# Head-row transfers of a stacked key/query tile: rows r, r+6, r+12, ... instead of sixteen neighbouring rows

## The chip, the cores and the metric

The kernel runs on one core of a Trainium2 chip. The metric is device time in microseconds (us) of one execution, as the median over several runs. Beside it there is one profiled execution, whose trace gives the start and length of every instruction and of every transfer. Engines are named as in the trace: PE (TensorE matmuls), PEld (TensorE weight loads), DVE (VectorE), ACT (ScalarE), POOL (GpSimd), SP (the queue from which most transfers are issued).

## The reference

Two parts run one after the other. The first is an attention with a complex decay: per batch (4) and head (8) a 48x48 complex state is carried over 768 steps. The second is a mixture of experts in which 3072 tokens are given to 8 experts, 384 tokens each, in the order of their gate logits.

```
mag = sqrt(a_re*a_re + a_im*a_im); scale = minimum(mag, 0.999) / (mag + 1e-06)
a_re_n, a_im_n = a_re * scale, a_im * scale
for t in range(S):                      # S = 768, per batch and head, D = 48
    new_re = ar * S_re - ai * S_im
    new_im = ar * S_im + ai * S_re
    S_re, S_im = new_re + outer(k[t], v[t]), new_im
    y[t] = q[t] @ S_re
x = y as [B*S, H*D]                     # 3072 x 384
logits = x @ w_gate; every token goes to its best expert that has room (384 each)
out[mask_e] = relu(x[mask_e] @ w1[e]) @ w2[e]
```

## The kernel before

The attention is computed in chunks of 128 steps. Three chunks are a group, two groups a batch, and there are eight groups (24 chunks). ACT and DVE first turn a group's decays into logarithms, running sums, and sines and cosines of the running angle (tile `CS`); keys and queries are scaled by the running decay (tile `kq`).

For each chunk, DVE then multiplies keys and queries by cosine and sine (`RK`, `RQ` in `turns`) and writes the result into tile `f`. In `f` a partition is one of 16 features and one of 8 heads (partition 8d+h), and along the partition lie 3 feature blocks x 2 (cosine part, sine part), each with 128 key columns, 128 query columns and one column `P0` with the decay of the whole chunk: 257 columns a chunk.

TensorE needs something else: for each head all 96 features (3 blocks x 2 parts x 16) along the partitions. This is tile `KQ`, 96 partitions x 8 heads x 257 columns per chunk. `stack` makes it with six transfers from on-chip memory to on-chip memory, issued on SP. Transfer r takes block r//2, part r%2 of all 128 partitions of `f` and puts it into 16 rows of `KQ`, each row holding its 8 heads one behind the other; this document calls it a head-row transfer. A group's three chunks are stacked in two packs: one chunk alone (six transfers of 16x8x257 elements) and the other two together (six of 16x8x514); in the last group the pack of two comes first. So there are 16 packs and 96 head-row transfers. `f` for a pack of two has one buffer, `KQ` has two.

Every reader of `KQ` either sums over its 96 rows or carries them along: `sc` (scores, key columns times query columns), `kp` (the key columns turned by TensorE, copied by ACT to `kt`, which makes the state update `U`), `W` (the state, `U` times the gate column, 96 rows), and the second half of `y` (state times query columns). DVE masks `sc` into `am`, and `am` times `V` is the first half of `y`. `xT`, `xp` and `x` bring `y` into token rows, which ACT's queue stores in DRAM (`xd`).

The order of the instructions on each engine is fixed ahead: `in_order` plays the list of operations through with estimated durations and emits them in that order; `hot` matmuls fill gaps in PE's estimated time. Each engine, and SP's queue, works in that order and waits where an operand is not there. A transfer on SP also waits for the transfer that used the same one of eight completion counters before it. The second part, the experts, begins after the last chunk and contains no head-row transfer.

Of the kernel before, what the change touches and what calls it, by code (L numbers as in the profile page):

```python
# [236 lines left out]
def attention(nc, real, tc, z, q, k, a_re, a_im, v_tok, xd, later):  # L237
# [29 lines left out]
    def op(key, eng, cost, prio, fn, deps=()):  # L267
        kind = key[0][0] if type(key[0]) is tuple else key[0]
        o = Op(eng, cost, fn, [made.get(d) for d in deps], prio)
        o.kind = kind + ("<" if prio < EARLY else ">" if prio >= LATE else "")  # L270
        if kind in LAGS:
            o.wait, o.lag = LAGS[kind]
        ops.append(o)
        made[key] = o
        return o

    def dve(n):
        return n / 960 + 0.1
# [19 lines left out]
    tiles = {}  # L298

    def get(name, gi, shape=None, p=ew, **kw):  # L300
        if (name, gi) not in tiles:
            tiles[name, gi] = p.tile(shape or [128, 3, T], F32, name=name, **kw)
        return tiles[name, gi]
# [128 lines left out]
    def pack(i):  # L432
        k = next(k for k, m in packs.items() if i in m)
        return k, i - packs[k][0], len(packs[k]), packs[k]

    def before(k, n):
        same = [x for x in packs if len(packs[x]) == len(packs[k])]
        at = same.index(k) - n
        return same[at] if at >= 0 else None

    def turns(i):

        gi, c = i // GC, i % GC
        piece = next(j for j, (lo, hi) in enumerate(cuts[gi]) if lo <= c < hi)
        t = slice(c * 128, c * 128 + 128)

        def X(*stages):
            return [(s_, gi, piece) for s_ in stages]

        pk, at, n, mates = pack(i)  # L450

        def ftile():
            return get(f"f{n}", pk, [128, 3, 2, n * 257], bufs=F_BUFS[n])[..., 257 * at:257 * at + 257]

        f_free = [("K", before(pk, F_BUFS[n]))]
        op(("P0", i), "dve", 0.1, i, lambda: v.tensor_copy(
            ftile()[..., 256], tiles["gc", gi][:, :, c, None].to_broadcast([128, 3, 2])), X("G4") + f_free)
        for m, name in enumerate(("RK", "RQ")):
            def rot(m=m):
                v.tensor_tensor(ftile()[..., 128 * m:128 * m + 128],  # L460
                                get("kq", gi)[:, m, :, t][:, :, None].to_broadcast([128, 3, 2, 128]),
                                tiles["CS", gi][..., t], op=OP.mult)
            op((name, i), "dve", dve(768), i, rot, X("T1", "T3", "G3" if m else "G5") + f_free)

        if at < n - 1:
            return

        def stack():
            KQ = get(f"KQ{n}", pk, [96, 8, n * 257], p=st, bufs=KC_BUFS[n])
            for r in range(6):  # L470
                nc.sync.dma_start(KQ[16 * r:16 * r + 16], tiles[f"f{n}", pk][:, r // 2, r % 2])
        deps = [(x, m) for m in mates for x in ("RK", "RQ", "P0")]
        for m in packs.get(before(pk, KC_BUFS[n]), ()):
            deps += [("MX", m), ("FL", m, 0), ("FL", m, 1), ("WM", m)]
        op(("K", pk), "dma", K_COST[n], i, stack, deps)

    nu = G * GC
# [970 lines left out]
```

## Time and profile before

| | |
|---|---|
| median of 3 runs | 640.8 us (640.6 to 641.47) |
| profiled execution, its own time | 643.34 us |
| its span, first to last instruction | 641.6 us |
| attention stage, from the first head-row transfer to the last state update | 38.7 to 347 us |
| experts | from about 347 us to the end |
| busy over the span | PE 81%, DVE 66%, ACT 43%, POOL 13% |
| mean granted TensorE clock | 0.846 of full speed |

The span is the profiled execution's; around it lie 1.7 us of the profiled execution's time. Shares of busy time over the whole span mix the two stages; the stage with the head-row transfers is the first.

### The profile page before, as it was taken

Reading aid. Unit: us, or ns where it says so; the run is one execution under the profiler, and the core shown is the slowest. Engines: PE = TensorE matmul, PEld = TensorE weight load, DVE = VectorE, ACT = ScalarE, POOL = GpSimd, SP = SyncE. Lnnn points to the kernel's source line nnn. Section 1 sums busy time; section 2 is a strip of 40 time slices with the busy share of each in tenths; the row PEclk is TensorE's granted clock in tenths of the full one; section 3 lists DMA queues with packets and bytes.
Section 4 is the critical chain, followed back from the end, with each engine's and each line's share of the span. In section 5 each row is a group of like instructions: output and inputs, shape, how many; then the busy total and the mean of one; then the engine's idle time right before and its main releaser. Section 6 shows DMA issues by size and latency. Waiting matters only on the chain.

```text
span 641.6 us, 9748 instructions
## 1 busy us (share of the span) xinstructions
PE 518.9 (81%) x3706; PEld 455.1 (71%) x3713; DVE 425.2 (66%) x1250; ACT 278.1 (43%) x426; POOL 84.3 (13%) x96
## 2 busy tenths in 40 slices
PE   0047988959689593987897599898999999999994
PEld 0017867757677573976786398477988898899994
DVE  8874766836658274574524757678899999895140
ACT  6882645746447372642421013323243434364140
POOL 2000000000000000000000021313323241451101
PEclk9995695956959587785859579799999999999998
DMA  8779496976969769295941154106342434391000
GB/s 260 219 104 175 111 158 194 143 192 132 153 195 135 200 139 148 95 117 93 119 68 38 35 201 186 61 25 229 111 166 104 167 120 152 134 363 46 26 13 37
DMA packets 41230, 86.04 MB, mean 134 GB/s; under 512 B 3809, under 2 KB 29921, under 8 KB 39137
## 3 DMA queue, kind: packets, MB, share of 16 engines
q1 hardware_dynamic: 31424, 42.55, 35.6%
q0 software_dynamic: 6304, 38.16, 17.9%
q10 hardware_dynamic: 3456, 4.72, 2.5%
q8 instruction: 29, 0.48, 0.3%
q14 instruction: 17, 0.13, 0.1%
HBM read 53.49 MB, written 9.44 MB: 98 GB/s over the span
## 4 chain that ended last, share of the span: by engine, by line
PE 43%; DMA 27%; DVE 12%; issue 8%; SPq 4%; ACT 3%; POOL 2%; POOLq 0%; DVEq 0%; ACTq 0%
PE acc L131 25%; DMA KQ<-f 19%; PE sc L131 5%; SPq L131 4%; PE y L131 3%; PE U L131 3%; DVE f L131 2%; PE kp L131 2%; DMA V<-in_v 2%; PE cnt L131 2%; ACT s L131 2%; PE xp L131 2%; DMA xd<-x 2%; DMA w1t<-in_w,eidx 1%; DMA s<-s 1%
## 5 line engine op out<-in xcount | busy, mean ns | idle before, releaser
L131 DVE TENSOR_TENSOR am<-sc,mask 128x512 f32<-128x512 f32 x48 | 32.7, 689 | 80.3 <-PE sc L131 80.3
L131 PE MATMUL sc<-KQ 96*128 96x128 f32 x384 | 67.6, 348 | 4.1 <-DMA KQ<-f 4.1
L131 PEld LDWEIGHTS sc<-KQ 96*128 96x128 f32 x384 | 64.4, 259 | 6.1 <-issue 5.8
L131 PE MATMUL kp<-ident,KQ 96*128 96x96 f32 x160 | 25.6, 322 | 53.0 <-DMA KQ<-f 39.1
L131 PEld LDWEIGHTS kp<-ident,KQ 96*128 96x128 f32 x160 | 22.1, 193 | 60.1 <-issue 57.4
L131 PE MATMUL hot<-cold 128*128 128x512 bf16 x113 | 28.6, 408 | 36.9 <-DVE cold L131 36.4
L131 ACT ACTIVATE hh<-acc 128x384 fp32r<-128x384 f32 x56 | 27.4, 491 | 63.2 <-PE acc L131 63.0
L131 PE MATMUL acc<-w2l,hh 128*128 128x384 f32 x168 | 54.1, 346 | 0.0
L131 PE MATMUL acc<-w2h,hh 128*128 128x384 f32 x168 | 53.7, 345 | 0.0
L131 PE MATMUL acc<-w2h,hl 128*128 128x384 f32 x168 | 53.5, 343 | 0.0
L131 PE MATMUL acc<-xl,w1h 128*128 128x384 f32 x168 | 51.4, 344 | 0.0
L131 PE MATMUL acc<-xh,w1h 128*128 128x384 f32 x168 | 51.3, 345 | 0.0
L131 PE MATMUL acc<-xh,w1l 128*128 128x384 f32 x168 | 51.2, 344 | 0.0
L131 PEld LDWEIGHTS <-cold 128*128 128x128 bf16 x120 | 12.6, 105 | 51.0 <-issue 35.7
L131 PE MATMUL y<-am,V 128*64 128x128 f32 x384 | 45.9, 337 | 0.0
L131 POOL DMA_INDIRECT out<-ot,idx x24 | 30.6, 1273 | 116.2 <-ACT ot L131 106.0
L131 PEld LDWEIGHTS U<-V,kt 128*96 128x96 f32 x320 | 41.9, 223 | 2.4 <-issue 1.9
L131 DVE TENSOR_TENSOR f<-kq,CS 128x768 f32<-128x768 f32 x48 | 42.6, 951 | 0.5 <-ACT CS L131 0.5
L131 PE MATMUL U<-V,kt 128*96 128x48 f32 x320 | 41.9, 301 | 1.0 <-DVE W L131 1.0
L131 ACT ACTIVATE kt<-kp 128x384 f32<-128x384 f32 x40 | 18.9, 489 | 54.7 <-PE kp L131 53.5
L131 DVE SCALAR_TENSOR_TENSOR hl<-acc,hh 128x384 fp32r<-128x384 f32 x56 | 30.4, 551 | 17.8 <-ACT hh L131 17.1
L131 DVE TENSOR_TENSOR ind<-m,thr 128x768 bf16<-128x768 f32 (+1 forms) x40 | 33.7, 848 | 8.5 <-PE thr L131 8.1
(198 smaller groups left out, 1179.7 us busy)
## 6 DMA issues: line engine op xcount, KB each, us to landing
KQ<-f SPq DMA_DIRECT2D x48, 257.0 KB, 10.6
KQ<-f SPq DMA_DIRECT2D x48, 128.5 KB, 4.6
V<-in_v SPq DMA_DIRECT2D x8, 576.0 KB, 13.8
kq<-in_k SPq DMA_DIRECT2D x8, 576.0 KB, 8.2
kq<-in_q SPq DMA_DIRECT2D x8, 576.0 KB, 8.4
xd<-x ACTq DMA_DIRECT2D x24, 192.0 KB, 3.5
ai<-in_a_im SPq DMA_DIRECT2D x6, 576.0 KB, 4.5
ar<-in_a_re SPq DMA_DIRECT2D x6, 576.0 KB, 3.9
```

The lines of the kernel that those rows point to most:

```text
L131: r = f(*a, **k)
```

## The change

The row order of `KQ` within a head changes. Transfer r wrote the 16 neighbouring rows 16r to 16r+15; now it writes the rows r, r+6, r+12, ..., r+90. Its source, its size, its place in the order and the queue it is issued on stay as they are, and so does every instruction on every engine, with its waits. The readers of `KQ` use all 96 rows, so the sums run over the same terms in another order of rows, and the state's rows are in the new order too.

```
--- before
+++ after
@@ -468,7 +468,7 @@
         def stack():
             KQ = get(f"KQ{n}", pk, [96, 8, n * 257], p=st, bufs=KC_BUFS[n])
             for r in range(6):
-                nc.sync.dma_start(KQ[16 * r:16 * r + 16], tiles[f"f{n}", pk][:, r // 2, r % 2])
+                nc.sync.dma_start(KQ[r::6], tiles[f"f{n}", pk][:, r // 2, r % 2])
```

## Rows read from the trace of the kernel before

**Rows 1.** The page: the span, and the chain of work that ended last by engine and line, with shares of the span.
```profile
span 641.6 us, 9748 instructions
...
PE acc L131 25%; DMA KQ<-f 19%; PE sc L131 5%; SPq L131 4%; PE y L131 3%; PE U L131 3%; DVE f L131 2%; PE kp L131 2%; DMA V<-in_v 2%; PE cnt L131 2%; ACT s L131 2%; PE xp L131 2%; DMA xd<-x 2%; DMA w1t<-in_w,eidx 1%; DMA s<-s 1%
```

**Rows 2.** The attention stage as one stretch: its length, busy time and number of instructions of PE, PEld, DVE, ACT and POOL, the granted clock, the busy share of the DMA engines (over 1 where packets overlap), GB/s.
```profile
38.70:347.00 308.30, 248.84 (x1892) 217.07 (x1897) 178.94 (x321) 149.99 (x191) 3.37 (x4) 0.73 0.77 138
```

**Rows 3.** The chain of waits between 225 and 300 us, in order of time, from the first issue of a cycle to the landing of its pair and on to the next `f`: start, us, what.
```profile
233.28 0.55 SPq L131
...
235.82 5.15 DMA KQ<-f
...
240.99 14.85 DMA KQ<-f
...
270.59 1.90 DVE f L131 x3
```

**Rows 4.** SP's queue, one row from 192 us and then between 228 and 282 us: start, us over which the x transfers were issued, what.
```profile
191.95 9.47 SPq L131 DMA_DIRECT2D KQ<-f  x12
...
233.28 8.26 SPq L131 DMA_DIRECT2D KQ<-f  x12
...
272.50 8.34 SPq L131 DMA_DIRECT2D KQ<-f  x12
```

**Rows 5.** Everything that writes or reads tile `KQ`: the 96 issues (shortest, median, longest in ns), the time from issue to landing, and from the page the median landing of the pair's transfers (257 KB) and of the single chunk's (128.5 KB).
```profile
L131 SPq DMA_DIRECT2D KQ<-f x96: 547/597/1265, 38.7 to 330.4; - x96
...
DMA to landing us min/median/max: 3.1/5.8/16.4
...
KQ<-f SPq DMA_DIRECT2D x48, 257.0 KB, 10.6
KQ<-f SPq DMA_DIRECT2D x48, 128.5 KB, 4.6
```

**Rows 6.** Three stretches (columns as in rows 2): one in which only head-row transfers of a pack of two move beside a store, one in which only loads of `kq` and `V` move, one with those of a pack of one.
```profile
242.00:254.00 12.00, 3.78 (x33) 3.40 (x32) 5.05 (x12) 3.23 (x6) 0.00 (x0) 0.80 1.08 116
257.00:260.00 3.00, 3.00 (x18) 3.00 (x17) 0.61 (x1) 2.82 (x4) 0.00 (x0) 0.50 1.05 370
235.00:240.00 5.00, 3.96 (x36) 2.63 (x35) 5.00 (x8) 4.64 (x7) 0.00 (x0) 1.00 1.09 131
```

**Rows 7.** The packets of the first and of the last of these stretches.
```profile
DMA packets 766, 1.39 MB, mean 116 GB/s; under 512 B 89, under 2 KB 114, under 8 KB 765
DMA packets 718, 0.66 MB, mean 131 GB/s; under 512 B 79, under 2 KB 718, under 8 KB 718
```

**Rows 8.** TensorE's groups of the attention stage that waited for head-row transfers: number, busy us, mean ns, idle us of the engine before them and who ended it.
```profile
L131 PE MATMUL sc<-KQ 96*128 96x128 f32 x384 | 67.6, 348 | 4.1 <-DMA KQ<-f 4.1
L131 PE MATMUL kp<-ident,KQ 96*128 96x96 f32 x160 | 25.6, 322 | 53.0 <-DMA KQ<-f 39.1 <-DMA V<-in_v 7.9 <-issue 6.0
```

**Rows 9.** The cycle from 233 to 273 us, and one row of the next, in order of time: start, us, engine, what, and in brackets the engine's idle time before it.
```profile
244.74 1.04 PE L131 MATMUL xp<-pick,xT 112*128 112x104 f32 x8
256.08 1.51 PE L131 MATMUL kp<-ident,KQ 96*128 96x96 f32 x8 [10.30 <-DMA KQ<-f]
257.39 1.97 PE L131 MATMUL sc<-KQ 96*128 96x128 f32 x8
259.15 2.69 PE L131 MATMUL U<-V,kt 128*96 128x48 f32 x16
259.39 0.69 DVE L131 TENSOR_TENSOR am<-sc,mask 128x512 f32<-128x512 f32 x1 [11.87 <-PE sc L131]
262.60 1.35 DVE L131 TENSOR_TENSOR kq<-kq,zi 128x1152 f32<-128x1152 f32 x1
263.10 0.64 PE L131 MATMUL y<-KQ,W 96*64 96x128 f32 x4
265.38 1.28 PE L131 MATMUL U<-W,ident 96*96 96x384 f32 x2
267.58 0.69 DVE L131 TENSOR_TENSOR am<-sc,mask 128x512 f32<-128x512 f32 x1 [3.63 <-PE sc L131]
269.15 1.08 PE L131 MATMUL sc<-KQ 96*128 96x128 f32 x8
270.06 1.48 PE L131 MATMUL U<-V,kt 128*96 128x48 f32 x16
270.59 1.82 DVE L131 TENSOR_TENSOR f<-kq,CS 128x768 f32<-128x768 f32 x2
272.19 0.39 PE L131 MATMUL y<-KQ,W 96*64 96x128 f32 x4
273.39 0.89 PE L131 MATMUL U<-W,ident 96*96 96x384 f32 x2
...
281.45 0.88 PE L131 MATMUL kp<-ident,KQ 96*128 96x96 f32 x8 [2.37 <-DMA KQ<-f]
```

**Rows 10.** Stretches of 3 us (columns as in rows 2) around the wait in that cycle, and around the one at 279 us.
```profile
245.00:248.00 3.00, 0.78 (x7) 0.61 (x6) 2.53 (x7) 1.54 (x2) 0.00 (x0) 1.00 1.07 113
248.00:251.00 3.00, 0.00 (x0) 0.00 (x0) 0.00 (x0) 0.00 (x0) 0.00 (x0) 0.69 1.08 123
...
263.00:266.00 3.00, 3.00 (x25) 2.44 (x22) 0.96 (x1) 0.51 (x2) 0.00 (x0) 0.50 0.00 0
266.00:269.00 3.00, 3.00 (x25) 2.74 (x24) 1.21 (x2) 2.29 (x3) 0.00 (x0) 0.96 0.02 5
...
278.00:281.00 3.00, 1.08 (x20) 0.84 (x16) 3.00 (x8) 0.90 (x2) 0.00 (x0) 1.00 1.14 124
281.00:284.00 3.00, 2.55 (x22) 2.55 (x23) 1.71 (x5) 1.94 (x4) 0.00 (x0) 0.88 1.09 114
```

**Rows 11.** From the list of who waits for whom in the whole kernel (us in total, times, longest) ACT's wait for the accumulating transfer `s<-s`; then this transfer: between 60 and 250 us its issues and its time to landing, and its last issue there, and at the end its two issues before 38 us, with their size and median us to landing.
```profile
ACT s L131 <- DMA s<-s: 25.9, 5, 7.6
...
L131 POOL DMA_DIRECT2D s<-s x4: 833/844/846, 80.9 to 198.6; - x4
...
DMA to landing us min/median/max: 12.2/14.5/15.8
...
198.61 0.85 POOL L131 DMA_DIRECT2D s<-s  x1 [38.67 <-ACT s L131]
...
s<-s POOLq DMA_DIRECT2D x2, 576.0 KB, 6.1
```

## The prediction

> **What bounds the kernel now.** I read the page first. The chain that ended last spends 19% of the span on one kind of transfer, the head-row transfers [rows 1]. No other item that belongs to the attention alone is above 5%, and the 25% of `acc` are the experts, in which nothing changes. So the question is what those transfers cost in the attention stage, 308.3 us long, in which DVE is busy for 178.9 us and PE for 248.8 us at a granted clock of 0.73 [rows 2].
>
> The chain of waits shows how the stage turns. DVE finishes `f`, SP issues twelve head-row transfers (first those of the single chunk, then those of the pair), the pair's data land, PE starts `kp` and `sc`, DVE masks, and 14.5 us after PE's start DVE begins the next `f` [rows 3, 9]. In the cycle that I follow, the first issue stands at 233.28, PE starts on the pair at 256.08, and the next first issue is at 272.50 [rows 4, 9]: 39.2 us, of which 22.8 lie between the issue and the landing of the pair.
>
> Then I asked why the landing takes 22.8 us. SP is not the reason: it has issued all twelve after 8.26 us [rows 4]. The twelve carry 96 rows x 8 heads x 771 columns x 4 bytes = 2.37 MB, in 22.8 us 104 GB/s. In stretches with nearly nothing but head-row transfers the 16 DMA engines are busy without a break and move 116 and 131 GB/s; loads, with the engines just as busy, 370 [rows 6]. It is not the length of the packets either: those of the single chunk are about half as long (0.66 MB in 718 packets against 1.39 MB in 766, 0.9 and 1.8 KB), and the rate is the same or a little better [rows 6, 7]. A rate in bytes that doesn't depend on the packet's length speaks for a place that all of them squeeze through. The source is 128 partitions; what is narrow is the destination, 16 neighbouring rows, written by all 16 engines at once.
>
> [...]
>
> **What the change costs and gives.** No instruction is added, removed or moved, and the bytes and the 96 issues of about 0.6 us [rows 5] are the same. What changes is the landing time.
>
> *Term 1, the waits for head-row transfers.* The new rate lies between 116 (nothing gained) and 370 GB/s (as the loads). The destination now resembles that of the loads, but only 96 partitions are written and both ends are in on-chip memory; I take the middle, 243. The pair's 1.58 MB then need 6.5 us. Its first issue comes 4.1 us after the cycle's first, and some 2 us are fixed (the shortest landing of all is 3.1 us [rows 5], of which 0.13 MB at 116 GB/s explain 1.1). So it lands 12.6 us after the cycle's first issue, instead of 22.8. The floor, set by SP, is the last issue at 7.7 plus 3.1, which is 10.8. Now what PE has to do meanwhile: its last work before the wait ends at 245.78, which is 12.5 us after the first issue [rows 9]. So the whole wait of 10.30 us goes in that cycle, and with 370 GB/s no more would go: PE itself is next. DVE, which idles 11.87 us here, would idle about 1.5. Over the stage, PE's idle time before the groups that need `KQ` is 53.0 + 4.1 = 57.1 us [rows 8]; the rows that name `V` or "issue" there belong to it, since the `V` load stands behind the head-row transfers in the same queue. In some cycles a microsecond or less will remain, and I take 54.
>
> *Term 2, TensorE's clock.* After the wait PE runs at 0.50, and it is back at 1.00 only at about 266 us, some 10 us of work later [rows 10]. What that costs is read from the same work at either level: eight `kp` 1.51 and 0.88 us, eight `sc` 1.97 and 1.08, `U` 2.69 and 1.48, four `y` 0.64 and 0.39, the carry of `U` 1.28 and 0.89 [rows 9]. On the path through the cycle: the first `sc` is ready after 1.9 instead of 3.3 us; DVE's five operations (4.9 us, from 259.39 to 263.95) are done at 6.5 instead of 7.9; PE, with `U` done at 3.4, `y` at 5.6 and the carry at 6.5, has the next half of `sc` at 7.6, where DVE's mask now starts at 11.5; from that mask to `f` DVE needs 3.0 us as before. So `f` begins 10.6 us after PE's start instead of 14.5: 3.9 us a cycle, 31 us over eight, if the clock doesn't fall. Whether it falls is the unknown: an idle time of 2.37 us was enough, with the sparse work before it, for a fall at about 283 us [rows 9, 10], and waits of one or two microseconds will remain where PE now hangs on DVE. Nothing below (no gain) and 31 above; I take half, 16.
>
> *What is late next.* The accumulating transfer `s<-s` lands 12.2 to 15.8 us after its issue in the stage, but in 6.1 before the first head-row transfer; ACT waits 25.9 us for it in all [rows 11]. It is in competition with the same engines and will land earlier too. If it stayed at 15.8 in the cycle whose first issue is at 191.95, it would land 22.5 us after that issue (it is issued 6.7 after it [rows 4, 11]), later than the pair, and ACT's and DVE's next steps would wait for it. There are four such cycles; I set this at nothing and keep 2 us in each, 8, for the range.
>
> *Sum.* 54 + 16 = 70 us. From the profiled execution's 643.3 us that gives 573.3; the median of the runs is 2.5 us lower than that execution, so 571. A stage of 238 us still holds DVE's 179 us of work.
>
> **The rivals.** (a) *The clock holds everywhere.* Then the waits go whole (57) and so do the 31: 88 us, 553. For it: after the change PE has work to its last instruction before the pair lands. Against it: DVE would be busy 179 of 220 us in fixed order, and each of its delays is an idle time for PE.
>
> (b) *The clock doesn't come back, or the rate rises only to about 170 GB/s.* The first gives 54 less the 8 of `s<-s`, so 46: 595. By the second the pair needs 9.3 us and lands at 15.4, nearly 3 us of wait stay in each of eight cycles, and the clock falls: 54 - 23 = 31, or 610. The middle is 602.
>
> (c) *The rate belongs to head-row transfers as such,* to the read of 2 KB pieces from eight partitions each, or to on-chip memory at both ends. Then the rows' order does nothing: 641, within 0.2%, which is about what a measurement of this kernel can tell from no change. For it: no other transfer of this kind stands in the trace. Against it: the same rate at half the packet length.
>
> (d) *Slower: SP pays for the stride.* If issuing 16 rows that lie apart takes longer than 16 neighbours, the queue becomes the bound. Eleven issues before the last one and its landing of 3.1 us reach the present 22.8 us at 1.8 us from one issue to the next, against 0.7 now; from there it is slower. At 2.0 a cycle would grow by 2.3 us, eight of them by 18: 659. For it: one issue of 1.27 us stands in the trace [rows 5]. Against it: that is the longest of 96, with a median of 0.6, and the number of rows is the same.
>
> **How the numbers follow.** Forecast (60 to 80 us gained) 0.40, (a) 0.25, (b) 0.24, (c) 0.06, (d) 0.05. Between (c) and a gain of over 0.2% there is little room, since a rate that rises at all shortens a wait on the path. The predicted time is that of the forecast, 571. The range reaches below to (a) with the order of the engines a little better used, 545, and above to the middle of (b), 602. That leaves out (c), (d), and a part of (b), together under 0.2. Faster 0.89, same 0.06, slower 0.05.
>
> **What the profile of the changed kernel would show.** Right: stretches of head-row transfers at 200 to 300 GB/s instead of 116; the median landing of the pair's transfers down from 10.6 us [rows 5] to about 6; SP's twelve issues still in about 8 us; PE's idle time before `kp` and `sc` down from 57 to under 10; first issues of cycles some 30 us apart instead of 39; the granted clock of the stage at 0.85 or more. The experts keep their length. Wrong: the same rate of 104 to 131 GB/s means (c); issues of over a microsecond mean (d); a high rate with the clock still at 0.50 after each landing means term 2 is nothing; a high rate with DVE waiting for ACT, and ACT for `s<-s`, means that the accumulating transfer took the place of the wait.

## The result, and the profile after

The median fell from 640.7 to 560.7 us (four runs between 552.9 and 566.0); the ratio is 0.871, with a 95% interval of 0.862 to 0.881. Ratios leave out runs more than 1.5% above the fastest of their kernel, here the one of 566.0 us; medians and ranges have all runs. The forecast was 571, between 545 and 602.

The page of the kernel after: the span, the chain of work that ended last by line, and at the end the issues of the head-row transfers with size and median us to landing.

```profile
span 558.5 us, 9748 instructions
...
PE acc L131 28%; PE sc L131 6%; SPq L131 6%; PE y L131 5%; DMA KQ<-f 4%; PE U L131 4%; DMA V<-in_v 4%; DVE f L131 2%; PE kp L131 2%; PE cnt L131 2%; ACT s L131 2%; DMA w1t<-in_w,eidx 2%; DMA s<-s 1%; PE thr L131 1%; PE xp L131 1%
...
KQ<-f SPq DMA_DIRECT2D x48, 257.0 KB, 6.2
KQ<-f SPq DMA_DIRECT2D x48, 128.5 KB, 2.4
```

Against [rows 1], the head-row transfers have gone from 19% of the chain to 4%; against [rows 5], the pair's transfers land after 6.2 us instead of 10.6, the single's after 2.4 instead of 4.6.

The attention stage as one stretch, from the first head-row transfer to the landing of the last stored chunk, first in the kernel before, then in the kernel after (columns as in rows 2: length; busy time of PE, PEld, DVE, ACT, POOL; granted clock; DMA; GB/s).

```profile
38.71:348.28 309.57, 249.97 (x1900) 218.13 (x1906) 178.93 (x321) 150.03 (x192) 3.37 (x4) 0.74 0.77 138
```

```profile
37.78:268.23 230.45, 207.46 (x1900) 178.97 (x1906) 177.35 (x321) 148.86 (x192) 3.37 (x4) 0.91 0.68 185
```

The stage is 79.1 us shorter. The rest of the span's 83.1 us is 0.9 before the stage and 3.0 in the experts (293.3 and 290.3 us). PE's account of the stage shows in which form the gain came: its idle time is the length less its busy time, 59.6 us before and 23.0 after, so 36.6 us less; its busy time is 42.5 us less with the same 1900 instructions, at a mean clock of 0.91 instead of 0.74. DVE and ACT do the same work in the same time, within 1%.

The groups of PE that wait for head-row transfers, in the kernel after (columns as in rows 8):

```profile
L131 PE MATMUL sc<-KQ 96*128 96x128 f32 x384 | 55.6, 304 | 2.3 <-DMA KQ<-f 2.3
L131 PE MATMUL kp<-ident,KQ 96*128 96x96 f32 x160 | 20.3, 273 | 17.2 <-DMA V<-in_v 11.5 <-DMA KQ<-f 5.7
```

Their idle time is 19.5 us instead of the 57.1 of [rows 8] (in the rows that name `V`, PE starts at most 0.4 us after the pair's last landing, so these waits belong here), and one `sc` takes 304 ns instead of 348, one `kp` 273 instead of 322.

Two waits that are left, in order of time, with the clock after each. The first fence has SP's issues and PE's first work on the pair; the second a stretch of 3 us ahead of the first wait and one after each.

```profile
186.17 8.08 SPq L131 DMA_DIRECT2D KQ<-f  x12
...
200.80 0.85 PE L131 MATMUL kp<-ident,KQ 96*128 96x96 f32 x8 [2.27 <-DMA KQ<-f]
...
215.65 8.12 SPq L131 DMA_DIRECT2D KQ<-f  x12
...
230.44 0.85 PE L131 MATMUL kp<-ident,KQ 96*128 96x96 f32 x8 [2.30 <-DMA KQ<-f]
```

```profile
195.00:198.00 3.00, 3.00 (x30) 2.98 (x29) 2.67 (x6) 1.59 (x4) 0.00 (x0) 1.00 1.04 218
...
204.00:207.00 3.00, 3.00 (x27) 2.91 (x28) 3.00 (x3) 1.76 (x2) 0.00 (x0) 0.50 0.59 187
...
231.00:234.00 3.00, 3.00 (x31) 3.00 (x30) 1.55 (x4) 3.00 (x5) 0.00 (x0) 1.00 0.20 70
```

PE starts on the pair 14.6 us after the cycle's first issue in the first cycle and 14.8 in the second, where it was 22.8 [rows 4, 9] (in four other cycles it starts later; why is told below); head-row transfers move at 218 GB/s while the pair is on its way, where it was 116 [rows 6]. And two waits of the same length, 2.27 and 2.30 us, end differently: after the first the clock falls to 0.50, after the second it stays at 1.00.

### The profile page after: what moved, and what is told of

It is laid out like the page before. It is cut to its first block, busy times and chain, and to the rows that moved or that the text cites. A ratio compares the mean times of both kernels' runs of the same rounds, so it can differ in the third digit from the quotient of the medians.

```text
span 558.5 us, 9748 instructions
## 1 busy us (share of the span) xinstructions
PE 473.5 (85%) x3706; PEld 414.3 (74%) x3713; DVE 423.4 (76%) x1250; ACT 276.8 (50%) x426; POOL 84.9 (15%) x96
## 4 chain that ended last, share of the span: by engine, by line
PE 51%; DMA 13%; DVE 13%; issue 8%; SPq 6%; ACT 4%; POOL 2%; POOLq 0%; ACTq 0%; DVEq 0%
PE acc L131 28%; PE sc L131 6%; SPq L131 6%; PE y L131 5%; DMA KQ<-f 4%; PE U L131 4%; DMA V<-in_v 4%; DVE f L131 2%; PE kp L131 2%; PE cnt L131 2%; ACT s L131 2%; DMA w1t<-in_w,eidx 2%; DMA s<-s 1%; PE thr L131 1%; PE xp L131 1%
## 5 line engine op out<-in xcount | busy, mean ns | idle before, releaser
L131 PE MATMUL hot<-cold 128*128 128x512 bf16 x113 | 27.4, 395 | 35.8 <-DVE cold L131 35.5
L131 PE MATMUL sc<-KQ 96*128 96x128 f32 x384 | 55.6, 304 | 2.3 <-DMA KQ<-f 2.3
L131 PEld LDWEIGHTS sc<-KQ 96*128 96x128 f32 x384 | 52.4, 217 | 4.0 <-issue 3.6
L131 PEld LDWEIGHTS <-cold 128*128 128x128 bf16 x120 | 12.2, 102 | 49.2 <-issue 33.2
L131 DVE SCALAR_TENSOR_TENSOR hl<-acc,hh 128x384 fp32r<-128x384 f32 x56 | 30.3, 550 | 17.8 <-ACT hh L131 17.1
L131 DVE TENSOR_TENSOR f<-kq,CS 128x768 f32<-128x768 f32 x48 | 42.5, 948 | 0.5 <-ACT CS L131 0.5
L131 ACT ACTIVATE ot<-acc 128x384 f32<-128x384 f32 x24 | 11.7, 489 | 58.0 <-PE acc L131 49.9
L131 PE MATMUL y<-am,V 128*64 128x128 f32 x384 | 39.6, 297 | 0.0
L131 PEld LDWEIGHTS U<-V,kt 128*96 128x96 f32 x320 | 32.8, 182 | 3.7 <-issue 3.4
L131 POOL DMA_INDIRECT w1t<-in_w,eidx x8 | 9.3, 1159 | 172.1 <-DVE of L131 129.1
L131 PE MATMUL U<-V,kt 128*96 128x48 f32 x320 | 33.5, 262 | 2.1 <-DVE W L131 2.1
L131 PE MATMUL kp<-ident,KQ 96*128 96x96 f32 x160 | 20.3, 273 | 17.2 <-DMA V<-in_v 11.5
## 6 DMA issues: line engine op xcount, KB each, us to landing
KQ<-f SPq DMA_DIRECT2D x48, 128.5 KB, 2.4
```

The lines of the kernel that those rows point to most:

```text
L131: r = f(*a, **k)
```

## Experiments

### The stacking alone on the chip

A kernel that does nothing but stack: sets of six transfers as for a pair, each set after the one before has landed, with different destination rows, queues, sources and destinations.

```
for r in range(6):
    queue.dma_start(d[rows(r)], src[:, r // 2, r % 2])    # 16x8x514
nc.vector.tensor_copy(src[0:96, :, :, 0], ...)           # waits for all six, holds the next set
```

> Left out: everything but the stacking; the output is zeros. Six transfers of 16x8x514 elements (1.58 MB), as for a pair, run alone, each set twice. kA sixteen neighbouring rows; kB every sixth; kC every fourth of rows 0 to 63 (four transfers), every second of 64 to 95 (two); kD every second within 32 rows; kE every third within 48; kM every fourth of rows 32 to 95 (four), every second of 0 to 31 (two); kF neighbours, alternately from two queues; kH, kI, kJ the rows of kA, kB, kM read from DRAM; kR written to DRAM. Theory D (destination rows set the rate): kA 13.5 us of data (116 GB/s), kH the same; kB about 7 (220 GB/s, as in the kernel after); kR well under 13.5. Theory T (the rate belongs to transfers from on-chip to on-chip memory): kH under 7, kB no better than kA. Theory Q (transfers follow too closely in one queue): kF half of kA. [...]

Stretches in the middle of the eleven sets (columns: length; busy time of DVE and POOL; clock; busy share of the DMA engines; GB/s). In order: kA neighbours, kB every sixth row, kC, kD every second, kE every third, kM mixed, kF neighbours from two queues, kH neighbours from DRAM, kI every sixth and kJ mixed from DRAM, and kR into DRAM.

```profile
6.00:18.00 12.00, 0.00 (x0) 0.00 (x0) 1.00 1.03 110
38.00:43.50 5.50, 0.00 (x0) 0.00 (x0) 1.00 1.09 228
57.00:62.50 5.50, 0.00 (x0) 0.00 (x0) 1.00 1.09 222
77.00:83.00 6.00, 0.00 (x0) 0.00 (x0) 1.00 1.07 218
97.00:104.00 7.00, 0.00 (x0) 0.00 (x0) 1.00 1.08 164
121.00:125.50 4.50, 0.00 (x0) 0.00 (x0) 1.00 0.95 256
137.50:148.00 10.50, 0.00 (x0) 0.00 (x0) 1.00 1.05 139
172.00:183.00 11.00, 0.00 (x0) 0.00 (x0) 1.00 1.00 118
214.00:219.50 5.50, 0.00 (x0) 0.00 (x0) 1.00 1.07 231
244.50:249.50 5.00, 0.00 (x0) 0.00 (x0) 1.00 0.96 253
269.00:272.50 3.50, 0.00 (x0) 0.00 (x0) 1.00 1.08 292
```

DVE's copy that waits for a whole set; the idle time in brackets is the set from its issue to its landing. Of kA, kB, kC, kD, kE and kM one each:

```profile
35.56 0.16 DVE L45 COPY src<-kA 96x6 f32<-96x6 f32 x1 [16.04 <-DMA kA<-src]
45.15 0.16 DVE L45 COPY src<-kB 96x6 f32<-96x6 f32 x1 [9.43 <-DMA kB<-src]
64.58 0.16 DVE L45 COPY src<-kC 96x6 f32<-96x6 f32 x1 [9.75 <-DMA kC<-src]
84.75 0.16 DVE L45 COPY src<-kD 96x6 f32<-96x6 f32 x1 [9.86 <-DMA kD<-src]
106.32 0.16 DVE L45 COPY src<-kE 96x6 f32<-96x6 f32 x1 [11.44 <-DMA kE<-src]
127.21 0.16 DVE L45 COPY src<-kM 96x6 f32<-96x6 f32 x1 [8.91 <-DMA kM<-src]
```

Theory D holds. With neighbouring rows the rate is 110 GB/s from on-chip memory and 118 from DRAM, with every sixth row 228 and 231, with the mixed rows 256 and 253, so it is not the source; into DRAM the same source moves at 292. Theory T, that the rate belongs to transfers within on-chip memory, has fallen. Theory Q has fallen too: two queues give 139 instead of 110, not twice as much.

The order of the destination rows thus sets the rate, but not by how far the rows are spread: kB spreads the sixteen rows of a transfer over 91 rows of the tile and kD over 31, and they differ by 4% (228 and 218 GB/s); kE spreads them over 46 and is slower than both, at 164. Nor do the rates follow the distance between one row and the next: a distance of one gives 110, two 218, three 164 and six 228, and kC and kM, both with distances of four and two but at other rows of the tile, move at 222 and 256. What it is in the place of the rows that sets the rate, no run shows. For kM the trace shows 256 GB/s, about 6.2 us for a set's data, and 8.9 for the set (8.1 for its second), of which SP's six issues of 0.60 us (median) are nearly half. What holds the rate there is not shown.

### Two other orders of rows in the whole kernel

```
-                nc.sync.dma_start(KQ[r::6], ...)
+                nc.sync.dma_start(KQ[32 + r::4] if r < 4 else KQ[r - 4:32:2], ...)
```

> The whole kernel with a third order of rows: transfers 0 to 3 write every fourth row of rows 32 to 95, transfers 4 and 5 every second row of rows 0 to 31. If the destination still limits the kernel after (210 to 240 GB/s), and these rows spread further, the pair's data land 2 to 3 us earlier in each cycle, some of the remaining falls of the clock go, and the time is 545 to 556. If the read of the source is what is left, or SP's issue, the time is that of the kernel after, 553 to 566.

557.9 us (554.9 to 563.9), ratio 0.867 (0.861 to 0.873): within the runs of the kernel after. The pair's median landing is 5.5 instead of 6.2 us, and PE's idle time before `kp` and `sc` 17.1 instead of 19.5. Little was gained at this place by this order. That its rows spread further, and the 2 to 3 us a cycle, were the author's estimate; alone on the chip the runs show 0.5 us a set (8.9 against 9.4; 1.3 in the second sets, 8.1 against 9.4).

```
+                nc.sync.dma_start(KQ[32 * (r // 2) + r % 2:32 * (r // 2) + 32:2], ...)
```

> The whole kernel with transfer r writing every second row of a block of 32 rows: spread over 32 partitions instead of 96. If what counts is that the rows lie far apart or reach many places, the rate falls back between 116 and 220 GB/s and the time lies between 575 and 620. [...]

569.7 us (568.5 to 577.8), ratio 0.892 (0.885 to 0.900): below the band of a rate that falls back, and 9 us above the kernel after. So rows that lie two apart within 32 rows bring most of the gain too, as alone on the chip (218 GB/s against 228), but the two kernels are not the same. The experiments on every third row and on the clock, below, come back to this.

### The clock without the landing

The kernel before, with its neighbouring rows, and extra matmuls on a constant tile in the waits for the pairs (`WARMTH` has their number for each of the eight pairs, in order):

```
+                for _ in range(WARMTH[len(warmed) - 1]):      # [13, 22, 33, 34, 38, 44, 20, 10]
+                    nc.tensor.matmul(hot, cold[:, :128], cold, start=True, stop=True)
```

> The kernel before, with its sixteen neighbouring rows, and before TensorE's first work on each pair 10 to 44 extra matmuls on a constant tile (2 to 9.5 us), about as long as the wait there was. The landing stays at 22.8 us after a cycle's first issue; only the clock can change. If a fall of the clock after the wait costs 3.9 us a cycle on the path, the time is 641 - 20 to 31, so 610 to 621. If the stage then merely waits for something else, 636 to 645.

621.8 us (619.9 to 622.9), ratio 0.970 (0.965 to 0.975): 20 us less than before, at the lower end of term 2. Its stage, all instructions and then the constant matmuls alone, and last the constant matmuls that the kernel before has of its own:

```profile
37.74:325.85 288.11, 263.44 (x2106) 205.88 (x2120) 178.52 (x321) 148.59 (x192) 3.37 (x4) 0.89 0.83 148
37.74:325.85 288.11, 74.14 (x314) 0.89 0.83 148
...
38.71:348.28 309.57, 26.31 (x108) 0.74 0.77 138
```

Without those 74.1 us PE is busy for 189.3 us. The same sum for the kernel before is 250.0 less 26.3 for its own constant matmuls, 223.7. PE's real work thus became 34.4 us shorter, but the stage only 21.5. Of the 12.9 us between, about 7 are extra matmuls that ran on after the pair had landed (in three cycles PE started on it 1.2, 3.6 and 2.4 us after the landing), so the clock is worth 20 us or more here. The rest fits PE finishing earlier ahead of a wait for a transfer, which only lengthens the wait. In the cycle followed in the prediction, PE's start on the pair to the next first issue took 11.7 us (238.10 to 249.77) instead of 16.4: 4.7 less, a little more than the 3.9 us worked out there.

```profile
238.10 0.85 PE L131 MATMUL kp<-ident,KQ 96*128 96x96 f32 x8 [1.14 <-DMA KQ<-f]
...
249.77 9.62 SPq L131 DMA_DIRECT2D KQ<-f  x12
```

### The clock after the change

The same with the kernel after, `WARMTH = [0, 0, 20, 8, 20, 9, 9, 4]`.

> The kernel after (every sixth row), and before TensorE's first work on the pairs of cycles 2 to 7 some extra matmuls on a constant tile (20, 8, 20, 9, 9, 4, at about 0.21 us each), as long as the waits that are left there (4.7, 2.0, 4.8, 2.3, 2.3, 1.1 us). If what is left of the gain hangs on the clock, which still falls after three or four of these waits, the stage's clock rises from 0.91 to 0.97 or more and the time is 545 to 553. If the waits themselves or DVE's 177 us of work in a stage of 230 hold it, 557 to 565.

Four runs between 540.9 and 559.4 us, median 549.9. In the profiled run (541.4 us) the stage, and the constant matmuls in it, are

```profile
38.26:249.99 211.73, 205.60 (x1977) 169.06 (x1976) 177.10 (x321) 148.08 (x192) 3.37 (x4) 0.99 0.74 202
38.26:249.99 211.73, 43.06 (x185) 0.99 0.74 202
```

The stage is 19 us shorter than in the kernel after, at a clock of 0.99, and DVE's 177 us now fill 84% of it. PE's work without constant matmuls is 162.5 us, against 182.3 in the kernel after (207.5 less 25.1 of its own); what is left of the stage is as long as there (49.2 and 48.1 us). In this profile the clock holds from 50 us to the end of the stage and falls only after it, at about 254 us. So in this run what was left of the waits cost by the clock after them. It is not held in every run: over the four, the mean clock was 0.969 in the two of 541 us and 0.95 in the two of 558 and 559.

> The third order of rows (every fourth row of rows 32 to 95, every second of 0 to 31), with extra matmuls in its own remaining waits (5, 0, 16, 10, 22, 7, 5, 0). If landing and clock both still count, 540 to 550, below every kernel so far. If the third order brings nothing but another draw of where the clock falls, it ends within 3 us of the kernel after kept warm.

542.1 us (540.7 to 550.7 over five runs), ratio to the kernel before 0.844 (0.837 to 0.850): the lowest median measured here, below both kernels, and outside the interval of the kernel after. Against the kernel after kept warm its best runs are equal (540.7 and 540.9), so the third order of rows by itself is not shown to bring anything.

### Pairs only, singles only

```
+                nc.sync.dma_start(KQ[r::6] if n == 2 else KQ[16 * r:16 * r + 16], ...)    # n == 1 in the second
```

> Only the pairs are stacked with every sixth row; the single chunks keep sixteen neighbouring rows. The two orders do not fit together, so the state sums are of other numbers; all work is done. By the rates seen alone on the chip (114 and 213 GB/s) the single's 0.79 MB take 6.9 us and the pair's 1.58 MB 7.4: the pair lands about 16.5 us after a cycle's first issue, 2 us later than in the kernel after. Waits of 2 us more in eight cycles and one or two more falls of the clock: 575 to 595. If the singles did not matter at all, 555 to 566.

584.7 us (579.7 to 587.5), ratio 0.908 (0.901 to 0.915). In the three cycles without the accumulating transfer `s<-s` [rows 11], of the seven that stack the single chunk first, the pair landed 16.5 to 17.3 us after the first issue.

> Only the single chunks are stacked with every sixth row; the pairs keep sixteen neighbouring rows. Again the state sums are of other numbers and all work is done. The single's data take 3.7 us and the pair's 13.8: the pair lands about 19.5 us after a cycle's first issue instead of 22.8. That is 3.3 us in eight cycles, 26 us, with the clock still falling after every wait: 610 to 622. If the first landing of a cycle counted as much as the last, under 600.

621.7 us (four runs between 621.5 and 625.3; a fifth took 792.1 us, at a mean clock of 0.57), ratio 0.969 (0.961 to 0.976). In the same three cycles the pair landed after 19.3 to 19.4 us. The pairs alone give 58 us and the singles alone 21, together 79, and the whole change gives 80. So the two shares add up, nearly in the ratio of their bytes (two to one would be 53 and 26). Both landings are close to those worked out ahead from the order of the data, 16.5 and 19.5 us: the singles matter because their data stand ahead of the pair's in the same engines.

### Every third row, and every second row kept warm

```
+                nc.sync.dma_start(KQ[48 * (r // 3) + r % 3:48 * (r // 3) + 48:3], ...)
```

> The whole kernel with transfer r writing every third row of a block of 48. Alone on the chip a pair's set then moves at 164 GB/s and lands after 11.4 us, against 16.0 for neighbouring rows (641 us) and 9.4 for every sixth (561). If the time follows the landing on a straight line, 641 - 80 x 4.6 / 6.6 = 585. If the clock sets a step, so that any wait long enough for a fall costs the whole 20 to 40 us, it lies above, 595 to 610.

583.5 us (576.7 to 587.7), ratio 0.911 (0.905 to 0.917): on the straight line. Landing of a set alone on the chip against the time of the whole kernel: 16.0 us and 641; 11.4 and 583.5; 9.9 and 569.7; 9.4 and 560.7; 8.9 (8.1 in the second set) and 557.9. Between the first and the fourth a microsecond of landing is worth 12 us, 1.5 in each of eight cycles. A set is a pair's; in the kernel the single's six transfers, half as many bytes, get faster with it, and the clock comes on top. These runs do not split the 1.5 between the two. On that line every second row lies some 5 us above every sixth, more than half of the 9 that were measured.

> Every second row of a block of 32, as in the kernel that took 569.7 us, with extra matmuls in the waits that were left there (11, 0, 17, 8, 4, 10, 11, 0). If that kernel is 9 us slower than the one with every sixth row only because the clock fell in other cycles (landings alone on the chip are 9.8 and 9.4 us), it now lies where that one lies when kept warm, 541 to 559. If its rows are slower in some way of their own, it stays 8 us or more above, 558 to 567.

562.3 us (555.1 to 568.0): the median lies in the second band, two of the four runs (555.1 and 558.3) in the first, and it is not settled. In its profile, of the run of 568.0, the waits had moved to other cycles than those whose lengths the extra matmuls were set by, and PE still waited 2.2, 3.0 and 2.7 us for pairs, each followed by a fall to 0.50; the stage's clock was 0.90. The clock was not held, and the remaining 4 us between every second and every sixth row stay open.

## Why the prediction was right, and where its steps were off

**What bounds the kernel** was right: the destination of the head-row transfers held the landing of the pair, and with it the stage. That the rate was no lower with packets half as long (116 GB/s at 1.8 KB, 131 at 0.9 [rows 6, 7]) was the observation that decided it, and the stacking alone confirmed it against rival (c) and theory Q. The 131 GB/s of [rows 6] was not reached there: alone, the old rows moved at 110. Rival (d) is refuted: SP's issues took 0.60 us (median) as before, and alone on the chip the longest with the new rows is 0.79 us against 0.68. Twelve of the 96 took 1.1 to 2.1 us, all in the four cycles told of next.

**Term 1 was mis-sized: 54 us were forecast, and PE's idle time fell by 37.6 (all idle time of the stage by 36.6).** The step that failed is the landing 12.6 us after a cycle's first issue. It rested on 243 GB/s, the middle between the two rows; the rate is 218 in the kernel after and 228 in the stacking alone. At 220 the same sum gives 13.3 us. In the three cycles in which SP's twelve issues took their 8.1 us the pair landed after 13.5 to 14.7 us, and PE started on it at 14.6 and 14.8 in the two shown above. In the four cycles between 60 and 186 us the issues took 10.3 to 12.7 us (in the one at 60 us, 2.9 of them were a wait for a store that had used the same completion counter) and the pair landed after 16.7 to 18.2. The forecast that the issues stay at 8 everywhere was read from one cycle; in the same four cycles of the kernel before they took 9.4 to 16.4. Two of the four in the kernel after, and the accumulating transfer issued in each:

```profile
86.57 12.67 SPq L131 DMA_DIRECT2D KQ<-f  x12
...
121.47 10.80 SPq L131 DMA_DIRECT2D KQ<-f  x12
...
90.75 0.85 POOL L131 DMA_DIRECT2D s<-s  x1 [24.84 <-DVE am L131]
125.87 0.84 POOL L131 DMA_DIRECT2D s<-s  x1 [34.27 <-ACT s L131]
```

The DMA queues between 92 and 98 us (packets, MB, share of the time of the 16 engines): q0 carries `s<-s`, q1 what SP issued.

```profile
q0 software_dynamic: 144, 0.59, 58.6%
q1 hardware_dynamic: 446, 0.74, 42.3%
```

The four cycles are those in which POOL issues `s<-s`, which takes 58.6% of the engines' time in the stretch shown, while the pair is on its way. PE started on the pair 17.6 and 18.5 us after the first issue in the two shown. The prediction set `s<-s` at nothing in the sum; on average the pair landed 3.4 us later with it than without. No run leaves `s<-s` out, so this is read from the traces alone. The other kernels show the same four cycles late, the kernel before by 1.8 us, the one with the mixed rows with PE's start on the pair 17.3 to 21.3 us after the first issue instead of 13.0 to 14.0, but for one cycle of the kernel with every second row: there `s<-s` was issued 7.5 us after the first issue, and the pair landed after 14.9. The 2 us in the cycles without `s<-s` and the 2 to 5 in three of these four explain what stayed of the waits; in the fourth PE still had work.

**Term 2 was mis-sized the other way: 16 us of at most 31 were forecast, and PE's busy time fell by 42.5.** The price of 3.9 us a cycle was near what was measured (4.7 in the same cycle of the kernel before kept warm). What the bound left out is that a full clock also shortens the work ahead of the next wait. In the kernel before, a part of that is taken up by the wait, which grows by as much, and the clock alone brings 20 us; once the wait is short, it counts too. That this is all of the 42.5 is argued, not shown. The two terms are therefore not independent. Their sum, 70 against 79 for the stage, came out closer than either because one was too large by 16 us and the other too small by 26: that part is luck.

**What is late next.** As a wait of ACT, `s<-s` came to nearly nothing, as forecast: it landed after 7.4 to 9.1 us instead of 12.2 to 15.8 [rows 11], and ACT's wait for it in the stage went to 1.4 us. What it cost was the later landing of the pair. Rival (a), the clock held everywhere at 553, meets the best run of the kernel after (552.9) in the number only: that run's mean clock is 0.938, as in the profiled run, where the clock falls to 0.50 after five waits in the stage. With extra matmuls that hold the clock the time is lower still (541). Rival (b) is refuted in both its forms: the rate is well above 170 GB/s, and the clock did come back. But the pair's landing in the four cycles with `s<-s` was later than the 15.4 us of its second form, for another reason.

**Of the signs named ahead:** rates of 200 to 300 GB/s, the pair's median landing near 6 us, the stage's clock above 0.85, an unchanged experts part and a first issue every 30 us (28.6 on average) came true. PE's idle time below 10 us (19.5) and twelve issues in 8 us everywhere did not.

## What to carry to other kernels

When transfers are slow with all engines busy, compare the rate in bytes at two packet lengths: if it is the same, look for a place that all packets share, and look at the destination rows of one transfer, not of the whole tile. Where the readers leave the order of rows free, try several orders in a kernel that does nothing but these transfers; here neighbouring rows moved at 110 GB/s, every third at 164, every second and every sixth at 218 and 228, and the mixed order at 256. Then look at what else uses the same engines while the transfers are on their way. A wait ahead of TensorE cost its own length here and the slow clock after it (4.7 us in the cycle followed), and the two have to be counted together: time saved ahead of a wait is taken up by it for as long as it lasts.

## What the runs showed of the hardware that was not expected

- Two queues writing neighbouring rows gave 139 GB/s instead of 110, far from double, although alternate transfers go to different rows.
- Waits of 2.27 and 2.30 us in the same kernel ended once with the clock at 0.50 and once at 1.00. The runs of the kernel after differ by 13 us (552.9 to 566.0), those of the kernel before in the same measurement by 2.6 (638.9 to 641.5); the mean clock goes with them only in part (0.938, 0.938, 0.924 and 0.921 at 552.9, 560.4, 561.1 and 566.0 us).
- Beside head-row transfers, `s<-s` with 0.59 MB took 58.6% of the DMA engines' time in 6 us, and 0.74 MB of SP's transfers 42.3%.
